# The last 96 MLP features in four column tiles, with a new static plan

## The chip, the cores and the metric

The kernel runs on one core of a Trainium2 chip. Times are microseconds (us) of device time for one launch. The engines are named as in the profile: PE (TensorE) for matrix products and PEld for its weight loads, ACT (ScalarE), DVE (VectorE), POOL (GpSimd) and SP (SyncE), which issues all the DMAs here.

## The reference

With x of 2048 tokens and 512 features, the kernel computes a gated mix of two branches:

```python
x = A_x                                                   # [1, 2048, 512]
g = sigmoid((x * gate_w).sum(-1, keepdims=True))
q, k, v = heads(x @ wqkv)                                 # 32 heads of 16
scores = q @ k.T * 16 ** -0.5                             # only 0 <= i - j < 256 is kept
a = (softmax(scores) @ v) @ wo
h = layernorm(x)                                          # over the features
u = gelu(h.T @ w1 + b1)                                   # [512, 1376], over tokens
y = (u @ w2 + b2).T                                       # [2048, 512]
out = g * a + (1 - g) * y
```

All inputs and outputs are bf16. The MLP mixes tokens: w1 takes the 2048 tokens to F = 1376 hidden features and w2 takes them back. 1376 is 10 times 128 and 96 left over; those 96 are what the change is about.

## The kernel before

**Work and tiles.** Tokens come in NT = 16 tiles of 128. Projections are made per block of 512 tokens and per group of 128 columns (tasks `k`, `q`, `v`). Attention goes by windows of 128 queries, j from -1 to 15; a window has score groups `s` (products of keys and queries, L904 and L924), exponentials `e` on ACT (L949), masks `m` on DVE or POOL (L956 to L988) and outputs `pv` (L1010) that DVE transposes and scales back into the token buffer `xo` (`n1`, `n2`, `nz`, `n3`, `n4`). Score groups of kind C hold two corners of 64 queries and need a mask over the whole tile, which POOL makes in two instructions. Outputs of kind B wait for the C mask too, and for VZ, copies of V that SP's DMAs `vz` put apart; there are three VZ buffers, so a `vz` waits until an earlier window's outputs are done.

The MLP's first half is a loop over NFC = 11 groups of 128 features (L1148): the chain `u{fc}` sums over the 16 token tiles into one bank of PSUM, with a part of w1 as weights and `h` (512 features of x) as the moving operand, and the task `ub{fc}` adds b1 and moves the bank to `ug`. The eleventh, `u10`, has only 96 rows: its 16 products take as long as the others'. One task `gelu` on ACT follows, in four instructions. The second half is a chain `y{t}` per token tile (L1191): 11 products of w2 and `ug` and then 4 of `xo` and `wo`, so that the attention's output projection lands in the same bank. The last tile is made as two halves, y15l and y15r. Task `f{t}` scales the bank by the gate into an output buffer `ot`, and `o{t}` stores it. The ring `ot` has three buffers, so `f` waits for the store three outputs back.

**How a product is issued.** `chain` (L635) cuts its list of products into tasks of two, named after their first index (`u10.4` holds products 4 and 5). A chain task is *flexible*: after a tiled task that is in the set THEN it issues every product as four matmuls of 32 columns, side by side in the array's four column tiles (three for u10's 96 rows); otherwise as one dense matmul:

```python
for c in range(0, rows, 32) if tiled[0] else [0]:
    z_ = c + 32 if tiled[0] else rows
    made.append(nc.tensor.matmul(
        buf(b)[c:z_, c0:c0 + w_], lhsT=lhsT[:, c:z_], rhs=rhs, start=(j == 0), stop=(j == n - 1),
```

Both forms stream the same 512 columns a product; the choice only saves changes of the array's mode. The modes are d (dense), p (128 by 32 tiles, also the outputs pv), s and c (score groups) and h (outputs of corners).

**What sets the order.** Nothing is scheduled at run time. PLAN (L190) lists every task of every engine in its order, written by a planner; `:` gives the buffers or banks that a task takes. `arrange` (L85) replays these lists with the tasks' costs and emits the program in the order of start times. An engine runs its list strictly in order, so a task that waits holds all behind it. That holds for SP's list too: an output store `o8` listed behind `vz12` is issued only when window 10's outputs have given their VZ buffer back.

**Small parts the change touches.** `small_loads` (L252 and on) brings b1, b2 and gate_w into the rows of one tile `biases` by four DMAs (task `bias`), PE transposes it (`biast`), and DVE copies its columns to b1c, b2c and gwc (`biasc`). `junk` is a scratch tile of 128 x 512 that the gate sums `gl` (L803) write and nobody reads.

Of the kernel before, what the change touches and what calls it, by code (L numbers as in the profile page):

```python
# [7 lines left out]
FP32 = mybir.dt.float32  # L8
# [76 lines left out]
def arrange(tasks):  # L85
# [21 lines left out]
    while len(order) < len(tasks):  # L107
# [84 lines left out]
        warm:5 xta0.0.1:6 xta0.0.0:4 warmb xta0.1.0:7 xta0.1.1:5 k1_0.0:0 k1_0.1 k0_0.0:3 k3_0.0:7 q1_0.0:1 k0_0.1  # L192
        q1_0.1 q1_0.2 q3_0.0:6 k1_0.2 k0_0.2 q3_0.1 k3_0.1 q1_0.3 k2_0.0:4 k0_0.3 q1_0.4 q0_0.0:5 q0_0.1 k1_0.3
        q0_0.2 q0_0.3 k0_0.4 q0_0.4 k1_0.4 k3_0.2 k3_0.3 k2_0.1 k2_0.2 k2_0.3 k2_0.4 k3_0.4 q3_0.2 q3_0.3 s1.B0:02
        k3_1.0:4 q2_0.0:5 q3_0.4 k3_1.2 q2_0.1 q0_1.0:7 q0_1.2 q2_0.2 q2_0.3 s0.A0:02 q2_0.4 v1.0:6 q3_1.0:4 v1.2
        q3_1.2 v0.0:7 s0.CNone:20 v0.2 v2.0:6 s-1.CNone:24 v2.2 v14.0:7 v14.2 s2.CNone:02 v12.0:6 biast:4 v12.2
        v13.0:5 v13.2 v3.0:7 s0.A1:02 v3.2 k2_1.0:5 k2_1.2 gate0:4 v5.0:6 v5.2 s1.B1:02 q1_1.0:4 k2_2.0:7 k2_2.2
        pv-1.0:0 v15.0:5 v15.2 q1_1.2 s1.A0:02 k3_2.0:6 k3_2.2 v10.0:7 v10.2 pv0.0:0 pv0.1 pv0.2 s1.A1:24 v8.0:6
        v8.2 v7.0:7 s2.A0:02 v7.2 v4.0:6 k0_2.0:5 v4.2 k0_2.2 k1_1.0:7 s1.CNone:02 k1_1.2 k0_1.0:6 k0_1.2 s2.B0:40
        pv1.0:2 pv1.1 v6.0:7 v6.2 q2_1.0:6 q2_1.2 pv1.2 s2.A1:40 pv1.3 pv1.4 k1_2.0:7 v11.0:6 k1_2.2 v11.2  # L200
        s3.CNone:40 v9.0:7 v9.2 u2.0:6 u2.2 s2.B1:42 u2.4 u3.0:7 u3.2 s3.B0:04 u3.4 u3.6 u3.8 u3.10 pv2.0:2 pv2.1
        s3.A1:04 u3.12 u3.14 u2.6 pv2.2 pv2.3 s3.A0:40 u2.8 u7.0:7 u7.2 s3.B1:24 u7.4 u2.10 u2.12 u7.6 s4.A0:02
        u7.8 u7.10 u7.12 u2.14 u7.14 s4.B0:04 pv3.0:2 q0_2.0:6 q0_2.2 pv3.1 pv3.2 pv3.3 s4.A1:04 q3_2.0:7 u0.0:6
        q3_2.2 s4.B1:20 u0.2 u0.4 u0.6 u0.8 s4.CNone:42 u0.10 u0.12 u10.0:7 s5.A1:40 u0.14 u10.2 u10.4 u10.6
        s5.B0:24 u10.8 u10.10 u10.12 s6.A1:02 u6.0:6 u10.14 pv4.0:4 pv4.1 u6.2 pv4.2 pv4.3 s6.A0:20 u6.4 u6.6 u6.8
        s5.B1:24 q1_2.0:7 q1_2.2 u6.10 u6.12 s5.CNone:20 u6.14 k3_3.0:7 k3_3.2 s5.A0:24 q2_2.0:6 q2_2.2 u5.0:7
        s6.CNone:02 u5.2 u5.4 u5.6 u5.8 s6.B0:40 u1.0:6 pv5.0:2 u1.2 pv5.1 pv5.2 pv5.3 s6.B1:40 u5.10 u1.4 u5.12
        u1.6 s7.A0:42 u5.14 u1.8 pv6.0:0 pv6.1 pv6.2 pv6.3 s7.B0:24 u1.10 u4.0:7 u4.2 s8.A0:02 u4.4 u1.12 u1.14
        u4.6 s7.A1:40 u4.8 k1_3.0:6 k1_3.2 s7.CNone:42 u4.10 u4.12 u4.14 q0_3.0:6 s8.B0:04 q0_3.2 u8.0:7 u8.2
        s8.CNone:20 u8.4 u8.6 u8.8 u9.0:6 s7.B1:24 u8.10 u8.12 u9.2 s8.B1:02 u9.4 u9.6 u9.8 u9.10 u8.14 s8.A1:04  # L210
        pv7.0:2 u9.12 u9.14 pv7.1 pv7.2 pv7.3 s10.A0:60 k2_3.0:4 q2_3.0:5 k2_3.2 q2_3.2 q1_3.0:6 k0_3.0:7 q3_3.0:4
        k0_3.2 q3_3.2 pv8.0:2 pv8.1 pv8.2 pv8.3 q1_3.2 y4.0:5 y0.0:4 y4.2 y0.2 y4.4 y0.4 y0.6 s10.B1:26 y0.8 y0.10
        y0.11 y4.6 y0.13 y4.8 s9.A0:02 y4.10 y4.11 y8.0:4 y8.2 s9.CNone:06 y8.4 y4.13 y8.6 s9.A1:20 y8.8 y8.10
        y8.11 y7.0:5 s9.B1:62 y8.13 y7.2 y7.4 y7.6 s11.B0:60 y7.8 y2.0:4 y7.10 y7.11 s9.B0:62 y7.13 y2.2 y2.4
        s10.A1:60 y9.0:5 y2.6 y2.8 pv9.0:2 pv9.1 pv9.2 pv9.3 s10.B0:60 y2.10 y2.11 y2.13 y9.2 s12.CNone:26 y9.4
# [24 lines left out]
        e10.B0.1 e12.CNone.0:1 e12.CNone.1 e12.A1.0:7 e12.A1.1 e10.CNone.0:6 e10.CNone.1 e11.B1.0:0 e11.B1.1  # L240
        e11.CNone.0:4 e11.CNone.1 e11.A0.0:9 e11.A0.1 e12.B1.0:5 e12.B1.1 e11.A1.0:6 e11.A1.1 e13.A1.0:8 e13.A1.1
# [41 lines left out]
def kernel(  # L283
# [861 lines left out]

    ub = []
    m1 = []
    for fc in range(NFC):  # L1148
        f0 = fc * P
        fsz = min(P, F - f0)  # L1150
        g, w0 = fc // 4, (fc % 4) * P
# [134 lines left out]
```

The softmax here doesn't subtract the row's maximum and nothing guards it: scores larger than these inputs give would overflow.

## Time and profile before

| what | value |
|---|---|
| median of 13 runs | 202.85 us (202.47 to 203.39) |
| the profiled execution: its own time | 202.79 us |
| its span, from the first to the last instruction | 201.0 us |
| granted PE clock, mean | 0.998 |
| instructions | 8987 |
| PE idle by stage: 0 to 10 us | 2.21 us |
| 10 to 140 us | 4.41 us |
| 140 to 160 us | 1.37 us |
| 160 to 190 us | 0.69 us |
| 190 to 201 us | 3.36 us |

The span is shorter than the time by 1.8 us, which lie before the first and after the last instruction. The profile names an instruction by engine and line; since most products come from `chain`, they all have L652, and one tells them apart by what they read: `h,wb` is a `u`, `ug,wb` and `wo,xo` are a `y`, `XT,wqkv` a `k` or `q`, `wqkv,XT` a `v`. Shapes such as `128*32 128x512` are weights (rows by columns) and the moving operand. In the groups, the numbers after the bar are busy time, the mean of one in ns, and the idle time of the engine ahead of them. In the waits, they are the sum, the number of times and the longest. The busy time of PE joins matmuls that overlap.

### The profile page before, as it was taken

The numbers are of one execution on the slowest core, as the hardware profiler recorded it, in microseconds if no ns is written. First come the engines' busy times: TensorE is split into PE (matmuls) and PEld (weight loads), VectorE is DVE, ScalarE is ACT, GpSimd is POOL, SyncE is SP. The second block draws the span as 40 slices with busy tenths as digits, with TensorE's granted clock in tenths as the row PEclk, the third lists the DMA queues.
The fourth block names the chain that finished last, engine by engine and source line by source line (L and its number), as shares of the span: only waits on it lengthen the run. The fifth ranks groups of instructions, "written<-read, shape, count | busy, mean of one in ns | idle before, by whom it ended". The sixth has DMA issues, their size and how long they took to land.

```text
span 201.0 us, 8987 instructions
## 1 busy us (share of the span) xinstructions
PE 188.9 (94%) x4025; PEld 93.7 (47%) x4059; DVE 155.7 (77%) x289; ACT 167.8 (83%) x194; POOL 74.8 (37%) x72
## 2 busy tenths in 40 slices
PE   7899998999999998999999999999998999999993
PEld 3543344343445445446444554334544354544572
DVE  3698959989989982696779688756708986798983
ACT  3278998899899897997899799899796989998651
POOL 6394557724024479226020150202481722007120
PEclk9999999999999999999999999999999999999999
DMA  6999545996023100001199780010030020111101
GB/s 169 274 275 224 134 107 143 362 282 226 3 65 114 33 0 18 18 3 32 37 330 410 262 262 5 0 57 0 31 100 29 29 70 18 54 34 46 43 29 55
DMA packets 23189, 22.02 MB, mean 110 GB/s; under 512 B 7566, under 2 KB 21262, under 8 KB 23150
## 3 DMA queue, kind: packets, MB, share of 16 engines
q1 hardware_dynamic: 23150, 21.44, 36.1%
q8 instruction: 32, 0.52, 1.1%
q14 instruction: 7, 0.06, 0.1%
HBM read 15.61 MB, written 2.10 MB: 88 GB/s over the span
## 4 chain that ended last, share of the span: by engine, by line
PE 82%; DMA 3%; issue 3%; SPq 3%; ACT 3%; POOL 3%; DVE 2%; DVEq 0%
PE pb L652 60%; PE ps L1010 11%; PE ps L924 9%; POOL XT L518 3%; DMA wqkv<-in_A_wqkv_dram 2%; PE ps L904 2%; ACT et L949 1%; DVE ot L423 1%; SPq L711 1%; DMA out_dram<-ot 1%; ACT XT L949 1%; SPq L710 1%; ACT VA L584 1%; SPq L436 0%; DVE XT L1090 0%
## 5 line engine op out<-in xcount | busy, mean ns | idle before, releaser
L949 ACT ACTIVATE et<-ps 128x1024 bf16<-128x1024 f32 (+1 forms) x102 | 95.9, 1001 | 14.2 <-PE ps L924 9.0
L518 POOL TENSOR_SCALAR_AFFINE_SELECT et<-et 128x1024 bf16<-128x1024 bf16 (+2 forms) x34 | 45.1, 1329 | 82.4 <-ACT et L949 49.1
L949 ACT ACTIVATE XT<-ps 128x1024 bf16<-128x1024 f32 (+1 forms) x52 | 49.4, 1011 | 4.0 <-PE ps L924 2.0
L652 PEld LDWEIGHTS <-wb 128*32 128x32 bf16 (+4 forms) x646 | 32.3, 97 | 37.5 <-issue 6.3
L652 PE MATMUL pb<-ug,wb 128*32 128x512 bf16 (+6 forms) x367 | 43.8, 369 | 2.3 <-issue 1.3
L652 PE MATMUL pb<-h,wb 128*32 128x512 bf16 (+2 forms) x260 | 41.3, 380 | 1.6 <-issue 1.6
L652 PE MATMUL pb<-XT,wqkv 128*128 128x512 bf16 (+2 forms) x176 | 30.6, 370 | 2.0 <-issue 1.1
L518 POOL TENSOR_SCALAR_AFFINE_SELECT XT<-XT 128x1024 bf16<-128x1024 bf16 (+2 forms) x11 | 16.6, 1510 | 29.5 <-ACT XT L949 25.0
L924 PE MATMUL ps<-QZ,KT 32*128 32x256 bf16 (+1 forms) x528 | 23.9, 262 | 0.1
L1010 PEld LDWEIGHTS <-VA 128*32 128x32 bf16 (+1 forms) x1056 | 20.4, 97 | 6.9 <-issue 3.2
L736 DVE TENSOR_TENSOR QZ<-pb,par 128x1024 bf16<-128x1024 f32 x16 | 19.4, 1214 | 5.2 <-PE pb L652 5.1
L423 DVE TENSOR_SCALAR ot<-pb,c,c 128x512 bf16<-128x512 f32 (+1 forms) x15 | 11.8, 785 | 11.8 <-PE pb L652 11.6
L1010 PE MATMUL ps<-et,VA 128*32 128x128 bf16 (+2 forms) x736 | 19.2, 217 | 0.2 <-ACT et L949 0.2
L652 PEld LDWEIGHTS <-wqkv 128*128 128x128 bf16 (+1 forms) x184 | 12.3, 97 | 14.4 <-issue 1.1
L1090 DVE STREAM_TRANSPOSE et<-ps 128x1024 f32<-128x1024 f32 (+1 forms) x12 | 14.4, 1203 | 5.8 <-PE ps L1010 5.2
L924 PEld LDWEIGHTS <-KT 32*128 32x128 bf16 x528 | 7.8, 92 | 20.8 <-ACT et L949 7.8
L652 PE MATMUL pb<-wo,xo 128*32 128x512 bf16 (+2 forms) x161 | 17.1, 375 | 0.2
L652 PE MATMUL pb<-wqkv,XT 128*128 128x512 bf16 x60 | 15.9, 380 | 0.6 <-issue 0.5
L985 DVE TENSOR_TENSOR et<-et,mask 128x1024 bf16<-128x1024 bf16 x17 | 13.2, 783 | 1.5 <-ACT et L949 1.5
L1010 PEld LDWEIGHTS <-VZ 128*32 128x32 bf16 x832 | 13.3, 98 | 0.9 <-issue 0.5
L752 DVE BATCH_NORM_STATS2 stats<-xo 128x6 f32<-128x512 bf16 x16 | 10.5, 677 | 2.5 <-DMA xo<-in_A_x_dram 2.5
L1125 DVE STREAM_TRANSPOSE xo<-zt 128x512 bf16<-128x512 bf16 (+1 forms) x17 | 11.4, 673 | 0.3
(76 smaller groups left out, 186.8 us busy)
## 6 DMA issues: line engine op xcount, KB each, us to landing
wb<-in_B_w_dram SPq DMA_DIRECT2D x8, 512.0 KB, 9.3
wb<-in_B_w_dram SPq DMA_DIRECT2D x2, 2048.0 KB, 8.0
out_dram<-ot SPq DMA_DIRECT2D x15, 128.0 KB, 2.4
VZ<-VA SPq DMA_DIRECT2D x26, 70.0 KB, 2.7
xo<-in_A_x_dram SPq DMA_DIRECT2D x3, 512.0 KB, 5.6
wb<-in_B_w_dram SPq DMA_DIRECT2D x4, 352.0 KB, 6.0
wqkv<-in_A_wqkv_dram SPq DMA_DIRECT2D x4, 256.0 KB, 5.3
wb<-in_B_w_dram SPq DMA_DIRECT2D x1, 1024.0 KB, 5.1
```

Of the source, the lines that this page charges most:

```text
L423: return nc.vector.tensor_scalar(out=out_, in0=in_, scalar1=scale, scalar2=bias, op0=ALU.mult, op1=ALU.add)
L518: return nc.gpsimd.affine_select(out=out_, in_=in_, pattern=[[0, n] for n in pattern] + [[step, HB]], compare_op=op, fill=0.0, base=base_, ...
L652: made.append(nc.tensor.matmul(buf(b)[c:z_, c0:c0 + w_], lhsT=lhsT[:, c:z_], rhs=rhs, start=(j == 0), stop=(j == n - 1), skip_group_check= ...
L736: lambda k=k, b=b: nc.vector.tensor_tensor(out=QZ[:, k, :, (i % NQ) * SB:(i % NQ + 1) * SB], in0=buf(b)[:, None, :].to_broadcast([P, 2, SB ...
L752: f"bs{t_}", {"DVE": 0.67}, lambda b=b, t_=t_: nc.vector.bn_stats(buf(b)[:], xo[:, t_, :]),
L904: made.append(nc.tensor.matmul(buf(b2[r // 2])[m_:m_ + HB, at:at + P], lhsT=keys(t_, k)[rows, a:a + HB], rhs=q[rows], start=True, stop=Tru ...
L924: made.append(nc.tensor.matmul(to[:, :, done:done + m], lhsT=keys(t_, k)[rows], rhs=q[rows], start=True, stop=True, tile_position=(32 * r, 0),
L949: lambda n_=n_: nc.scalar.activation(out=shape(buf(e)[:, n_ * 1024:(n_ + 1) * 1024]), in_=shape(buf(b2[n_])), func=ACT.Exp, scale=SCALE),
L985: return nc.vector.tensor_tensor(out=view, in0=view, in1=mask[:, "AB".index(x), None, :].to_broadcast([P, n_, HB]), op=ALU.mult)
L1010: return lambda: nc.tensor.matmul(to(), lhsT=v() if callable(v) else v, rhs=buf(e)[rows, col:col + n], start=first, stop=last, tile_positi ...
L1090: lambda: nc.vector.transpose(out=view(buf(tr).bitcast(FP32)), in_=view(buf(o))), [last], takes=[tr], uses=[o],
L1125: return nc.vector.transpose(out=to, in_=src)
```

## The change

The eleventh group leaves the loop and is made by hand. Its 96 features are three groups of 32. Column tiles 0, 32 and 64 of the array each take one group and stream only the first 384 of the 512 columns; the fourth tile, at 96, which had nothing to do before, makes the last 128 columns of all three groups, one after another, into different columns of the same bank. So a step has six matmuls. Eight tasks of two steps stay in "p" mode always. The bank then has the last quarters in partitions 96 to 127, so DVE moves it out in four instructions, and the 96 biases are needed once more, in rows of 32 that lie at columns 96 to 127 of `biases`: one more small DMA, and b1c has 14 columns.

The ring `ot` gets `junk` as a fourth buffer, which comes free when the last `gl` has run. And all five lists and THEN are written anew: nearly every task has a new place or bank, and some have a new engine.

The core of the diff (of the lists, only stretches that the prediction speaks of):

```diff
 PLAN = dict(
     PE="""
...
-        q3_2.2 s4.B1:20 u0.2 u0.4 u0.6 u0.8 s4.CNone:42 u0.10 u0.12 u10.0:7 s5.A1:40 u0.14 u10.2 u10.4 u10.6
-        s5.B0:24 u10.8 u10.10 u10.12 s6.A1:02 u6.0:6 u10.14 pv4.0:4 pv4.1 u6.2 pv4.2 pv4.3 s6.A0:20 u6.4 u6.6 u6.8
...
-        y0.11 y4.6 y0.13 y4.8 s9.A0:02 y4.10 y4.11 y8.0:4 y8.2 s9.CNone:06 y8.4 y4.13 y8.6 s9.A1:20 y8.8 y8.10
-        y8.11 y7.0:5 s9.B1:62 y8.13 y7.2 y7.4 y7.6 s11.B0:60 y7.8 y2.0:4 y7.10 y7.11 s9.B0:62 y7.13 y2.2 y2.4
-        s10.A1:60 y9.0:5 y2.6 y2.8 pv9.0:2 pv9.1 pv9.2 pv9.3 s10.B0:60 y2.10 y2.11 y2.13 y9.2 s12.CNone:26 y9.4
...
+        u0.2 q3_2.0:6 q3_2.2 s4.B0:42 u0.4 u0.6 u0.8 u0.10 s4.CNone:04 u10.0:6 u0.12 u0.14 u10.2 s6.A0:20 u10.4
+        u10.6 u10.8 u10.10 s5.B1:42 u6.0:7 u6.2 u10.12 u6.4 s6.B0:40 u10.14 u6.6 pv4.0:2 pv4.1 pv4.2 pv4.3 s5.A0:04
...
+        y0.13 y4.6 y4.8 s9.A0:04 y8.0:7 y8.2 y4.10 y4.11 s9.B0:02 y4.13 y8.4 y8.6 s10.CNone:40 y7.0:6 y8.8 y8.10
+        y7.2 s9.CNone:42 y8.11 y8.13 y7.4 y7.6 s9.B1:40 y7.8 y2.0:7 y2.2 s11.CNone:24 y7.10 y7.11 y7.13 y2.4
+        s10.B0:02 y2.6 y2.8 pv9.0:4 pv9.1 pv9.2 y2.10 pv9.3 s10.A1:20 y9.0:6 y2.11 y2.13 s10.B1:42 y9.2 y9.4 y9.6
...
     POOL="""
...
-        m8.B1 m9.A0 m11.B0 m10.A1 m10.B1 m12.C m11.C m13.A1 m12.A0 m14.C m15.ANone
...
+        m8.A0 m8.B1 m9.C m10.A1 m11.C m10.B0 m10.B1 m11.B1 m11.A1 m12.B0 m12.A0 m12.A1 m13.C m15.ANone
...
     SP="""
...
-        x0.0 x0.2 wqk0 wqk1 wqk2 wqk3 x1.4 xt1 wv x2.8 bias xt3 x3.12 vs0 w1_20 xt2 vs2 vz2:0 vs1 gw w1_10 w1_21
...
-        w2_2 wo vz9:0 o4 o0 o2 vz11:0 vz12:2 vs13 o8 o7 o1 o5 o10 vz13:0 o3 o11 vz14:1 o6 o12 o9 o13 o14 o15l o15r
...
+        x0.0 x0.2 wqk0 wqk1 wqk2 wqk3 x1.4 xt1 wv bias xt3 w1_02 x2.8 vs0 x3.12 xt2 w1_03 w1_12 vs1 w1_13 w1_00
...
+        w2_2 vz13:2 o0 o4 vz9:1 vz10:0 o8 o7 o2 o9 o1 vz11:1 vz12:0 o5 vs13 o10 vz14:1 o3 o11 o12 o6 o13 o14 o15l
...
     mask = sb.tile([P, 7, HB], BF16, name="mask")
     par = sb.tile([P, 2], FP32, name="par")
     gwc = sb.tile([P, 4], BF16, name="gwc")
-    NB = NFC + NT + 4
+
+    N1 = NFC + 3
+    NB = N1 + NT + 4
     biases = sb.tile([NB, P], BF16, name="biases")
     gwr = sb.tile([P, D], BF16, name="gwr")
     junk = sb.tile([P, D], BF16, name="junk")
-    b1c = sb.tile([P, NFC], FP32, name="b1c")
+    b1c = sb.tile([P, N1], FP32, name="b1c")
     b2c = sb.tile([P, NT], FP32, name="b2c")
     mv = sb.tile([P, NT, 2], FP32, name="mv")
     rstd = sb.tile([P, NT], FP32, name="rstd")
...
     ztr = ring("zt", 2, [P, D], BF16)
     rdr = ring("rd", 2, [P, 32], FP32)
     otr = ring("ot", 3, [P, D], BF16)
+
+    otr.tiles.append(junk)
+    otr.avail.append(None)
+    jb = Buf(otr)
+    jb.index = 3
     vzr = Ring("vz", [VZ[:, i] for i in range(NVZ)])
 
     def buf(b):
...
             nc.sync.dma_start(
                 biases[NFC - 1:NFC, 0:F - (NFC - 1) * P], B_b1[(NFC - 1) * P:F].rearrange("(o p) -> o p", o=1)
             ),
-            nc.sync.dma_start(biases[NFC:NB - 4, :], B_b2[:].rearrange("(t p) -> t p", p=P)),
+            nc.sync.dma_start(
+                biases[NFC:N1, P - 32:P], B_b1[(NFC - 1) * P:F].rearrange("(g p) -> g p", p=32)
+            ),
+            nc.sync.dma_start(biases[N1:NB - 4, :], B_b2[:].rearrange("(t p) -> t p", p=P)),
             nc.sync.dma_start(biases[NB - 4:NB, :], gate_w.rearrange("(t p) -> t p", p=P)),
         ]
 
...
         keep(mask[HB:P, 6, :], mask[HB:P, 6, :], [], "F")
 
     k2 = add("masks", {"POOL": 4.2}, masks)
-    dbias = add("bias", {"SP": 1.5}, small_loads, [k0], lat=2.5)
+    dbias = add("bias", {"SP": 1.8}, small_loads, [k0], lat=2.5)
     bb = bank("xt")
     bt = add(
         "biast", {"PE": 0.12},
...
     )
 
     def bias_columns():
-        nc.vector.tensor_copy(out=b1c[:], in_=buf(bb).bitcast(BF16)[:, 0:NFC])
-        nc.vector.tensor_copy(out=b2c[:], in_=buf(bb).bitcast(BF16)[:, NFC:NB - 4])
+        nc.vector.tensor_copy(out=b1c[:], in_=buf(bb).bitcast(BF16)[:, 0:N1])
+        nc.vector.tensor_copy(out=b2c[:], in_=buf(bb).bitcast(BF16)[:, N1:NB - 4])
         return nc.vector.tensor_copy(out=gwc[:], in_=buf(bb).bitcast(BF16)[:, NB - 4:NB])
 
     k3 = add("biasc", {"DVE": 0.5}, bias_columns, [bt], uses=[bb])
...
                         out=junk[:], in0=xo[:, t_, :], scalar=1.0, in1=gwr[:], op0=ALU.mult, op1=ALU.mult,
                         accum_out=ez[:, t_:t_ + 1],
                     ),
-                    [dx[t_], dgw], two=True,
+                    [dx[t_], dgw], uses=[jb], two=True,
                 ))
             lready += gt
             gm = add(
...
 
     ub = []
     m1 = []
-    for fc in range(NFC):
+    for fc in range(NFC - 1):
         f0 = fc * P
-        fsz = min(P, F - f0)
+        fsz = P
         g, w0 = fc // 4, (fc % 4) * P
         mms = [(w1[g][:, t_, w0:w0 + fsz], h[:, t_, :], fsz) for t_ in range(NT)]
         b, t = chain(f"u{fc}", mms, dw1[g] + hready, "u")
...
             lambda b=b, fsz=fsz, fc=fc: affine(ug[:fsz, fc, :], buf(b)[:fsz, :], None, b1c[:fsz, fc:fc + 1]),
             [t, k3], uses=[b],
         ))
+
+
+
+    bl = bank("u")
+    W3 = 3 * D // 4
+    gl, wl = (NFC - 1) // 4, ((NFC - 1) % 4) * P
+
+    def emit_last(t_):
+        return [
+            nc.tensor.matmul(
+                buf(bl)[to:to + 32, c0:c0 + w], lhsT=w1[gl][:, t_, wl + 32 * n:wl + 32 * n + 32], rhs=h[:, t_, a:a + w],
+                start=(t_ == 0 and n == first), stop=(t_ == NT - 1), tile_position=(0, to), skip_group_check=True,
+            )
+            for n, to, c0, a, w, first in
+            [(n, 32 * n, 0, 0, W3, n) for n in range(3)] + [(n, 96, n * P, W3, P, 0) for n in range(3)]
+        ]
+
+    last = None
+    for t_ in range(0, NT, 2):
+        last = add(
+            f"u{NFC - 1}.{t_}", {"PE": 0.33}, lambda t_=t_: emit_last(t_) + emit_last(t_ + 1),
+            dw1[gl] + hready if last is None else [last], takes=[bl] if last is None else [],
+            uses=[] if last is None else [bl], mode="p", ins=24,
+        )
+    m1.append(last)
+
+    def move_last():
+        made = []
+        for to, n, c0, a, w in [(0, 96, 0, 0, W3)] + [(32 * n, 32, n * P, W3, P) for n in range(3)]:
+            at, col = (0, NFC - 1) if n == 96 else (96, NFC + to // 32)
+            made.append(nc.vector.tensor_scalar(
+                out=ug[to:to + n, NFC - 1, a:a + w], in0=buf(bl)[at:at + n, c0:c0 + w],
+                scalar1=b1c[at:at + n, col:col + 1], scalar2=None, op0=ALU.add,
+            ))
+        return made
+
+    ub.append(add(f"ub{NFC - 1}", {"DVE": 1.35}, move_last, [last, k3], uses=[bl]))
 
     cuts = [(0, 3), (3, 7), (7, NFC - 1)]
 
```

## The prediction

> **What bounds the kernel now.** I read the busy shares first, then the chain that ended last by engine, then who TensorE (PE) waited for.
>
> ```profile
> PE 188.9 (94%) x4025; PEld 93.7 (47%) x4059; DVE 155.7 (77%) x289; ACT 167.8 (83%) x194; POOL 74.8 (37%) x72
> ```
> ```profile
> PE 82%; DMA 3%; issue 3%; SPq 3%; ACT 3%; POOL 3%; DVE 2%; DVEq 0%
> ```
> ```profile
> PE pb L652 <- issue: 4.4, 28, 0.2
> PE pb L652 <- DVE ot L423: 0.9, 1, 0.9
> PE ps L1010 <- POOL XT L518: 0.4, 1, 0.4
> ```
>
> PE is busy for 188.9 of 201.0 us and is 82% of the chain, so array time saved anywhere after the first loads comes off the end, unless another engine is late next. Only two waits in the middle exceed 0.3 us. The 4.4 us of "issue" are 28 pieces of 0.16 us: such a stretch lacks exactly one matmul (5 records in 1.24 us after the gap, 6 in 1.40 us without one), so I take them as missing records, not time to win.
>
> Next, the chain in order of time, which gives prices.
>
> ```profile
> 71.63 2.61 POOL XT L518
> 74.30 2.46 POOL XT L518
> 76.80 0.58 PE ps L1010 x44
> ...
> 80.71 1.84 PE pb L652 x32
> ...
> 82.94 1.41 PE pb L652 x24
> ...
> 162.43 1.36 PE ps L1010 x128
> ```
>
> A dense product over 128 rows in "p" mode is four matmuls side by side, so x32 is 8 steps and x24 is 6. The two differ by 0.43 us over 2 steps: **0.215 us a step of 512 columns**, and 1.84 - 8 x 0.215 = **0.12 us to enter a mode**. Dense stretches give the same (1.83 us for 8, 1.40 us for 6; 0.11 us entry). The last line is one block's outputs: 128 matmuls, 3072 columns on each of the four column tiles, 3072 / 512 x 0.215 = 1.29 us, so almost all of it is streaming. The first lines show pv4.1 held by the two halves of a POOL mask.
>
> The groups with shapes kept apart give the object of the change and a row like its new one:
>
> ```profile
> L652 PE MATMUL pb<-h,wb 128*96 128x512 bf16 x14 | 3.5, 382 | 0.0
> L1010 PE MATMUL ps<-et,VZ 128*32 128x64 bf16 x384 | 6.9, 193 | 0.0
> ```
>
> The timeline shows the other wait:
>
> ```profile
> 149.18 6.24 SPq L1216 DMA_DIRECT2D out_dram<-ot  x3
> ...
> 151.20 0.81 DVE L423 TENSOR_SCALAR ot<-pb,c,c 128x512 bf16<-128x512 f32 x1 [5.14 <-PE pb L652]
> ...
> 152.07 0.60 PE L652 MATMUL pb<-ug,wb 128*128 128x512 bf16 x2 [0.94 <-DVE ot L423]
> ```
>
> The 151.20 line is f9, although y9 had been finished since about 149.6. It needs output buffer 2, whose store o8 was queued on SP behind vz11, vz12 and vs13 and went at 149.18 (f8 was done at 144.08); stores land after 2.4 us. PE then waits for f9's bank with y5.
>
> **What the Trainium skill says.**
> - "TensorEngine Tiling (Array Packing)", Key Properties: tiles work independently, and a change of tiling mode drains the array. The trace agrees: 0.11 to 0.12 us an entry.
> - The same page, Restrictions: column tiling excludes Fast Weight Load. So would three short matmuls in a row on one tile show their weight loads? In the blocks' outputs each tile takes new weights every 64 columns, 27 ns, and still streams at 1.29 of 1.36 us: loads of 32 columns are hidden there.
> - "TensorE: Matmul & The Clock Gate", Step-by-step: weight loads are pulled ahead of running matmuls when they go to the background buffer, matmuls stay in order. PEld's 97 ns loads beside uninterrupted PE agree.
> - "SBUF — State Buffer", SBUF: two separate sides: VectorE and GpSimd take a shared port pair as an exclusive lock. The mask pair took 5.12 us at 71.63, beside VectorE work, and 4.29 us at 146.18, where VectorE was nearly idle; that fits.
>
> **The change, part by part.**
>
> *Array time of u10.* Before: 16 steps of 512 columns (14 dense, 2 in three column tiles), 16 x 0.215 = 3.45 us. After: each step has 384 columns on tiles 0 to 2 and three times 128 on tile 96, so 384 columns on every tile: 384 / 512 x 0.215 = 0.162 us, 2.59 us in all. Gain **0.86 us**. Lower bound of the cost is 2.59. Upper: each of the three loads on tile 96 shows its 97 ns, 3 x (54 + 97) = 0.45 us a step, 7.25 us. I take the low end because of the 27 ns above.
>
> *Mode entries.* u10 must now run in "p". I counted runs of equal mode in the two PE lists: 171 become 173 (d 58 to 56, p 32 to 36). 4 x 0.12 - 2 x 0.11: **+0.25 us**.
>
> *Instructions.* u10 has 96 pairs of load and matmul instead of 20, and 81 other steps are tiled instead of 74: about 240 more instructions on 8084. The output blocks issue 256 in 1.36 us without a wait in the trace, against u10's 192 in 2.6 us. I take 0; the bounds are 0 and 0.3 us.
>
> *Moving u10 out.* One ACT instruction (0.69 us) becomes four on DVE: from the ot rows, 0.81 us for 512 columns and 0.54 for 256, I estimate 0.67 + 3 x 0.35 = 1.7 us. DVE is 77% busy, and gelu is far behind u10, with five more u groups between: 0 on the path. Without that cover, 1 us. Other copies change sides (ACT gives ten and takes seven; DVE gives three masks net to POOL): a few us on engines with slack, 0.
>
> *Bias.* The fifth small DMA is one more issue of about 0.3 us on SP, ahead of xt3, x2.8, vs0, x3.12 and xt2. But bias now goes before x2.8 (0.5 us) and so xt3 leaves no later than before, at about 12.7 us. xt2, after vs0 as before, leaves at about 21.3 us; its first user v10 comes at about 28.3 us by adding up the list, against a landing of 26.4 (traffic ended 5.1 us after issue before) to 29.4 (8.1, the longest transpose). I take 0, bounds 0 and 1.1. The wider b1c copy is 3 columns: nothing.
>
> *Fourth output buffer.* junk is free once the gl sums are done, long before the first output. f5, f7, f12 and f15l use it, and on SP o8, o7, o2, o9 and o1 now stand ahead of vz11, vz12 and vs13. The store that held f9 goes before those waits: **-0.94 us**. Bounds: -0.94 and 0, if PE merely waits elsewhere. Behind vz12, which waits for pv10, there is now o5, whose buffer is next needed by f12: covered by over 10 us.
>
> *The moved POOL mask.* m4.C stays; between s4.C and pv4.1 there are now 12 steps of u0 and u6 (2.59 us), u10 (2.59), three score groups (0.99), pv4.0 (0.22) and six entries (0.7), 7.1 us, against 24 steps (5.17), the same groups and pv4.0 and four entries (0.46), 6.8 us, before. **-0.25** of the 0.41, bounds -0.41 and 0. But m9.C moves from DVE (about 1.3 us) to POOL (4.3 to 5.1). From the end of s9.C to pv9.1 the new list has 25 steps (5.38), s9.B1, s11.C and s10.B0 with their entries (1.04), pv9.0 (0.22) and four other entries (0.45): 7.1 us. The mask needs 0.13 + 1.94 (two exponentials) + 0.06 + 4.3 to 5.1 = 6.4 to 7.25 us. I take **+0.2 us**, with ACT prompt; bounds 0 and 2.1, if ACT lags a pair.
>
> *All the rest planned anew.* Streaming (608 products, 60 + 17 score groups, 16.8 us of outputs) comes to about 166.6 us by these prices, 171 entries to 20; PE's 190.9 us from 6.80 to 197.7 leave some 4 us of waits, of which 1.35 are the two named. A new order keeps the same total work but breaks the pairs of wait and cover that the old one had. I put **+0.9 us** for new small waits, an estimate: three quarters of the 1.19 us of waits that I take out. Bounds 0 and 3. The start (first wqkv piece at 6.80) and the tail after pv15 (15 half-width products and y14's last four, 2.5 us, cover the DVE's 2.3 us from pv15 to y15's last inputs) are alike.
>
> *Sum.* 202.79 - 0.86 + 0.25 - 0.94 - 0.25 + 0.20 + 0.9 = **202.1 us**, against the profiled execution's own 202.79 (span 201.0 and 1.8 around it); the median of the runs, 202.85, is 0.06 from it. The runs spread over 0.9 us, so a change under about 0.2% (0.4 us) can't be told from none.
>
> **The rivals.**
> - *The new order has few waits of its own:* only the terms with a place count, 202.1 - 0.9 = **201.2**. For it: the longest PE wait goes. Against it: ACT is 19.15 of 20 us busy from 120 to 140 us; little slack for a list that reshuffles everything. 10%.
> - *A wash:* new waits of 1.7 us, not 0.9, eat all, **202.9**. For it: some 2.6 us of small waits exist even in the present order. 22%.
> - *Slower: m9.C on POOL decides.* Right after gelu (4.7 us and two table loads of 1.28 on ACT) the exponentials e9.A0, e9.B0, e10.C, e9.C come at a rate of one pair (1.94 us) per some 2 us of PE work. If ACT is one pair behind at s9.C, the mask ends 1.94 us later and pv9.1 waits 2.1 us instead of 0.2: 202.1 + 1.9 = **204.0**. It makes the kernel slower by over 0.4 us from a lag of about 1.2 us. For it: ACT nearly full in that stage. Against it: before, ACT waited for PE (0.43 us) at 127.46, so it had caught up. 25%.
> - *The fourth tile serves no purpose:* tile 96's loads show (7.25 us instead of 2.59), **206.8**. Against it: the 27 ns rows. 3%.
>
> **How the numbers follow.** Likeliest at 202.1 (between 201.4 and 202.4): 40%. Faster by over 0.2%: 40 + 10 = 50%; within: 22%; slower: 25 + 3 = 28%. The range runs from 200.9 (the first rival, less the 0.3 us by which entries and pv9 may cost less) to 204.2 (the third, plus the rest of pv4's wait), leaving out the last and the tails, under 2 in 10. Faster holds the most, but not by much; the likeliest case's own range is 201.4 to 202.4.
>
> **What would show it.** In the changed profile, u10's chain pieces: 12 matmuls per two steps in 0.33 us right, 0.9 us if loads show. PE's list of waits should have no DVE ot entry near 150 us; a POOL mask entry at L1010 near pv9, over 1 us, is the third rival. If PE is busy for about 0.6 us less yet the span isn't shorter, the new order's waits have it, and the idle time per stage tells where. I am wrong if the sum of PE's idle time in the middle grows by more than 1.5 us.

## The result, and the profile after

The median of 11 runs is **205.37 us** (204.75 to 207.06) against 202.94 us for 48 runs of the kernel before on the same chip: a ratio of **1.013, interval 1.0113 to 1.0147**. The kernel became slower by about 2.6 us; I had forecast 202.1 us, faster, with a range to 204.2. Executions that were disturbed (a lower clock, or a time well above the fastest of the same kernel) are left out of the ratios but not of the medians; in e1 below they are three of six, and its trace is of one of them. The profiled execution took 205.06 us (span 203.3), 2.27 us more than before's 202.79.

The page after, busy shares and the chain by engine:

```profile
PE 190.5 (94%) x4150; PEld 95.1 (47%) x4180; DVE 158.3 (78%) x292; ACT 166.7 (82%) x191; POOL 79.7 (39%) x75
...
PE 71%; DVE 15%; DMA 6%; issue 3%; POOL 2%; ACT 1%; SPq 0%; POOLq 0%
```

PE held 82% of the chain before and DVE 2%. Now DVE holds 15% and DMA 6%: some 30 us of the chain ran through VectorE and 12 us through transfers. The busy shares hardly show it (DVE 77 to 78%). PE's waits after the start:

```profile
PE pb L662 <- issue: 3.8, 24, 0.2
PE ps L934 <- ACT et L959: 1.6, 3, 0.6
...
PE ps L1020 <- DMA VZ<-VA: 0.8, 1, 0.8
PE pb L662 <- DVE QZ L746: 0.5, 1, 0.5
PE ps L934 <- DVE ug L429: 0.3, 1, 0.3
...
PE pb L662 <- DVE ug L429: 0.2, 1, 0.2
```

Both waits that I had taken out are gone from this list: no `ot` and no POOL entry. New are the score groups (L934) that wait for ACT, one transfer of VZ, and DVE entries.

u10 itself is as forecast. The groups of after, with shapes apart:

```profile
L1179 PE MATMUL pb<-h,wb 128*32 128x128 bf16 x48 | 3.5, 220 | 0.0
L1179 PE MATMUL pb<-h,wb 128*32 128x384 bf16 x48 | 3.5, 328 | 0.0
```

The timeline of PE in after:

```profile
71.04 1.52 PE L1179 MATMUL pb<-h,wb 128*32 128x384 bf16 x48
72.50 0.40 PE L934 MATMUL ps<-QZ,KT 32*128 32x256 bf16 x8
```

Forty-eight matmuls are eight steps, and the next group starts 1.46 us after the first of them. Less one mode entry of 0.12 that is 1.34 us, so 0.16 to 0.17 us a step, without loads that show.

**Where the time came from.** For both kernels I summed the work ahead of every score group with the prediction's prices and compared it with the times at which the groups started. What the clock says beyond the work is called lost. The entries are estimates: the prices are rounded, so a change in the last column may be off by 0.2 to 0.3 us.

| stretch (us in after) | lost before | lost after | change |
|---|---|---|---|
| ahead of the first score group | 6.81 | 6.55 | -0.26 |
| to s4.C (68.7) | 1.02 | 0.50 | -0.52 |
| s4.C to s5.A1 (85.8); in before, s4.C to s6.A0 (78.6) | 0.88 | 2.90 | **+2.02** |
| from there to s10.A0 (117.0) | 0.29 | 1.79 | **+1.50** |
| s10.A0 to s15.B (192.5) | 1.65 | 1.39 | -0.26 |
| after s15.B | | | +0.37 |
| work (prices) | | | -0.60 |

The sum is +2.25 of the 2.27 us. The work, by the same prices, fell as forecast (-0.61). Two stretches make the kernel slower. The busy column is no help: PE's busy time *rose* by 1.6 us with less work. I put this down to the ends of matmuls, which the profile models, so that part of a wait counts as busy. Its idle time from 10 to 190 us grew by only 1.15 us (6.48 to 7.63).

**First stretch, 72 to 86 us.** The timeline of after, first DVE's part:

```profile
72.12 1.92 DVE L1117 TENSOR_TENSOR zt<-et,rd 128x512 bf16<-128x512 f32 x1
73.97 0.70 DVE L1135 STREAM_TRANSPOSE xo<-zt 128x512 bf16<-128x512 bf16 x1
74.70 1.86 DVE L1117 TENSOR_TENSOR zt<-et,rd 128x512 bf16<-128x512 f32 x1
76.60 0.71 DVE L1135 STREAM_TRANSPOSE xo<-zt 128x512 bf16<-128x512 bf16 x1
77.23 1.69 DVE L1200 TENSOR_SCALAR ug<-pb,b1c 96x384 bf16<-96x384 f32 x4
```

POOL's part, the two halves of m4.C:

```profile
71.39 4.64 POOL L528 TENSOR_SCALAR_AFFINE_SELECT XT<-XT 64x2048 bf16<-64x2048 bf16 x2 [0.29 <-ACT XT L959]
```

ACT's part, the exponentials e5.B1 and e6.B0:

```profile
74.14 1.94 ACT L959 ACTIVATE et<-ps 128x1024 bf16<-128x1024 f32 x2 [1.04 <-DVE zt L1117]
76.66 1.94 ACT L959 ACTIVATE et<-ps 128x1024 bf16<-128x1024 f32 x2 [0.58 <-DVE zt L1117]
```

And PE's, the score groups s6.B0, s5.A0 and s5.B0:

```profile
75.22 0.40 PE L934 MATMUL ps<-QZ,KT 32*128 32x256 bf16 x8 [0.58 <-ACT et L959]
...
78.65 0.40 PE L934 MATMUL ps<-QZ,KT 32*128 32x256 bf16 x8 [0.38 <-ACT et L959]
...
81.09 0.40 PE L934 MATMUL ps<-QZ,KT 32*128 32x256 bf16 x8 [0.63 <-ACT et L959]
```

Read it from below. PE's score groups s6.B0, s5.A0 and s5.B0 wait for exponentials. The exponentials e5.B1 (74.14) and e6.B0 (76.66) wait for DVE's `zt` products: these are n31 and n33, which read the et buffers 3 and 0 that e5.B1 and e6.B0 are to fill. In the kernel before, the same operation took 0.69 us twice (69.51 and 71.56, in the fence below); here it takes 1.92 and 1.86 us, 2.4 us more in all. POOL's mask m4.C has two halves, 71.39 to 73.51 and 73.57 to 76.03; n31 ends 0.54 us after the first and n33 0.53 us after the second. Behind them on DVE come ub10, u10's four moves (77.23), and the next products. The kernel before, DVE:

```profile
69.51 0.69 DVE L1107 TENSOR_TENSOR zt<-et,rd 128x512 bf16<-128x512 f32 x1
...
71.56 0.69 DVE L1107 TENSOR_TENSOR zt<-et,rd 128x512 bf16<-128x512 f32 x1
...
73.57 1.20 DVE L1107 TENSOR_TENSOR zt<-et,rd 128x512 bf16<-128x512 f32 x1
78.85 1.25 DVE L1090 STREAM_TRANSPOSE XT<-ps 128x1024 f32<-128x1024 f32 x1 [4.08 <-PE ps L1010]
```

Before, one product met the mask (1.20) and DVE then stood idle for 4.08 us. The windows from 70 to 85 us (length; DVE's busy time and instructions; clock, DMA share, GB/s), in the kernel before:

```profile
70.00:85.00 15.00, 9.09 (x20) 1.00 0.05 12
```

and in the kernel after:

```profile
70.00:85.00 15.00, 14.66 (x28) 1.00 0.02 4
```

So DVE has next to no idle time left here, and 2.4 of its 14.66 us are the two products' lengthening.

**Second stretch, 112 to 117 us.** The chain of after:

```profile
104.13 0.37 SPq L1231
...
104.55 10.25 DMA VZ<-VA
...
114.85 0.74 PE ps L1020 x44
```

SP's queue in the timeline of after:

```profile
98.90 5.61 SPq L1231 DMA_DIRECT2D wb<-in_B_w_dram  x2
104.55 0.52 SPq L720 DMA_DIRECT2D VZ<-VA  x1
```

vz7, two copies of 70 KB, was issued behind two w2 loads of 2 MB each and landed 10.25 us later; pv7 waited for it, and a late ub8 then held s10.A0. Before, vz7 went ahead of the w2 loads: its first copy left at 91.28 us and landed at 93.83. SP's queue in the kernel before:

```profile
91.28 0.46 SPq L710 DMA_DIRECT2D VZ<-VA  x1
...
99.59 12.62 SPq L1184 DMA_DIRECT2D wb<-in_B_w_dram  x3
```

### The profile page after: what moved, and what is told of

Same layout as the page of the kernel before. It is cut to its first block, busy times and chain, and to the rows that moved or that the text cites. A ratio compares the mean times of both kernels' runs of the same rounds, so it can differ in the third digit from the quotient of the medians.

```text
span 203.3 us, 9231 instructions
## 1 busy us (share of the span) xinstructions
PE 190.5 (94%) x4150; PEld 95.1 (47%) x4180; DVE 158.3 (78%) x292; ACT 166.7 (82%) x191; POOL 79.7 (39%) x75
## 4 chain that ended last, share of the span: by engine, by line
PE 71%; DVE 15%; DMA 6%; issue 3%; POOL 2%; ACT 1%; SPq 0%; POOLq 0%
PE pb L662 52%; PE ps L1020 9%; PE ps L934 7%; DMA VZ<-VA 5%; DVE zt L1117 3%; DVE junk L814 2%; POOL et L528 2%; PE ps L914 2%; DVE QZ L746 2%; DVE xo L1135 1%; DMA xo<-in_A_x_dram 1%; DVE ug L429 1%; DVE et L1100 1%; DVE rd L1108 1%; DVE ug L1200 1%
## 5 line engine op out<-in xcount | busy, mean ns | idle before, releaser
L528 POOL TENSOR_SCALAR_AFFINE_SELECT et<-et 128x1024 bf16<-128x1024 bf16 (+3 forms) x34 | 45.8, 1358 | 89.9 <-ACT et L959 51.2
L959 ACT ACTIVATE XT<-ps 128x1024 bf16<-128x1024 f32 x50 | 48.3, 1024 | 4.7 <-PE ps L934 3.6
L662 PEld LDWEIGHTS <-wb 128*32 128x32 bf16 (+2 forms) x713 | 30.7, 96 | 34.5 <-issue 7.5
L662 PE MATMUL pb<-ug,wb 128*32 128x512 bf16 (+4 forms) x404 | 44.8, 370 | 0.8 <-issue 0.6
L662 PE MATMUL pb<-h,wb 128*32 128x512 bf16 (+1 forms) x295 | 38.4, 380 | 1.4 <-issue 1.4
L528 POOL TENSOR_SCALAR_AFFINE_SELECT XT<-XT 128x1024 bf16<-128x1024 bf16 (+1 forms) x14 | 20.8, 1488 | 21.4 <-DVE et L1104 6.3
L1100 DVE STREAM_TRANSPOSE et<-ps 128x1024 f32<-128x1024 f32 (+1 forms) x15 | 17.7, 1178 | 12.4 <-PE ps L1020 9.3
L934 PE MATMUL ps<-QZ,KT 32*128 32x256 bf16 (+1 forms) x528 | 24.0, 262 | 1.9 <-ACT et L959 1.6
L934 PEld LDWEIGHTS <-KT 32*128 32x128 bf16 x528 | 8.0, 92 | 22.2 <-ACT et L959 13.0
L430 DVE TENSOR_SCALAR ot<-pb,c,c 128x512 bf16<-128x512 f32 (+1 forms) x12 | 9.3, 779 | 9.5 <-PE pb L662 9.5
L662 PE MATMUL pb<-wqkv,XT 128*128 128x512 bf16 (+1 forms) x66 | 15.8, 380 | 0.6 <-issue 0.6
L1117 DVE TENSOR_TENSOR zt<-et,rd 128x512 bf16<-128x512 f32 (+1 forms) x15 | 14.4, 959 | 0.3
```

The lines of the kernel that those rows point to most:

```text
L430: return nc.vector.tensor_scalar(out=out_, in0=in_, scalar1=scale, scalar2=bias, op0=ALU.mult, op1=ALU.add)
L528: return nc.gpsimd.affine_select(out=out_, in_=in_, pattern=[[0, n] for n in pattern] + [[step, HB]], compare_op=op, fill=0.0, base=base_, ...
L662: made.append(nc.tensor.matmul(buf(b)[c:z_, c0:c0 + w_], lhsT=lhsT[:, c:z_], rhs=rhs, start=(j == 0), stop=(j == n - 1), skip_group_check= ...
L934: made.append(nc.tensor.matmul(to[:, :, done:done + m], lhsT=keys(t_, k)[rows], rhs=q[rows], start=True, stop=True, tile_position=(32 * r, 0),
L959: lambda n_=n_: nc.scalar.activation(out=shape(buf(e)[:, n_ * 1024:(n_ + 1) * 1024]), in_=shape(buf(b2[n_])), func=ACT.Exp, scale=SCALE),
L1100: lambda: nc.vector.transpose(out=view(buf(tr).bitcast(FP32)), in_=view(buf(o))), [last], takes=[tr], uses=[o],
```

## Experiments

**Theory.** The two stretches are the loss: vz7 queued behind w2, and DVE late between 72 and 86 us because products on DVE that read two SBUF tiles wait for POOL's mask and hold et buffers. **Rivals:** u10's new form costs time in itself (its 152 more instructions, its moves on DVE); or DVE simply has too much work there, mask or not. A side question is whether the fourth output buffer was worth its 0.94 us. All ratios are to the kernel before, run on the same chip beside them.

### vz7 ahead of w2

```diff
-... w2_0 w2_1 vz7:2 vz8:1 w2_2 ...
+... vz7:2 vz8:1 w2_0 w2_1 w2_2 ...
```

> The changed kernel with vz7 and vz8 issued ahead of w2_0 and w2_1 on SP. Theory C (pv7.1's wait is the 70 KB of vz7 standing behind 4 MB of w2 in the DMA queues, 10.2 us from issue to landing): vz7 lands before 103 us, PE's 0.81 us wait goes, 204.5 us, 0.8 to 1.1 under the changed kernel's 205.4; some 0.4 us stay, for s10.A0 needs u8's bank cleared. Rival D (pv7 waits for something else that ends at the same time, a mask or an exponential): no change, 205.4.

Measured: 203.27 us, ratio **1.0062 (1.004 to 1.0084)** against after's 1.013: 1.4 us less, where 0.8 to 1.1 had been expected. The wait for VZ is gone from PE's list, and the loss ahead of s10.A0 fell from 1.54 to 0.40 us. What stays there is the wait for ub8. This part of the theory is shown.

### The mask m4.C and the DVE products: five runs

m4.C from POOL to DVE, behind n33:

> The changed kernel with the mask m4.C (4.6 us in two POOL instructions) made on DVE behind n33 (1.2 us). Theory E (between 72 and 86 us PE waits for ACT, ACT for buffers that DVE gives back late, and DVE is late because POOL's mask holds the shared port while n31, n33 and nz4 want it, 1.92, 1.86 and 0.98 us instead of 0.69, 0.69 and 0.2): n31 and n33 take 0.7 us, 1.5 to 2.2 us of the 2.8 us of waits go, 203.2 to 203.9. Rival F (DVE simply has too much to do there, ub10 among it): 1.2 us more for DVE, 205.4 to 206.5.

Measured: 204.3 us, 1.0116 (1.0083 to 1.0149), which can't be told from after's 1.013. The timeline of this kernel has n31 and n33:

```profile
72.85 0.67 DVE L1117 TENSOR_TENSOR zt<-et,rd 128x512 bf16<-128x512 f32 x1
...
74.18 0.69 DVE L1117 TENSOR_TENSOR zt<-et,rd 128x512 bf16<-128x512 f32 x1
```

So it is the mask on POOL that lengthens the two products, as the theory has it. The first loss fell from 0.65 to 0.27 us, but new waits for DVE (0.6 at the gate sums) took its place. What the lengthening costs stays open here, since the mask now adds 1.2 us to DVE.

So I made the mask short instead, on top of vz7 early:

```diff
-return [keep(view[HB * i:HB * i + HB], view[HB * i:HB * i + HB], [32], "DF"[i]) for i in range(2)]
+w = 1 if j == 4 else 32
+return [keep(view[HB * i:HB * i + HB, 0:w], view[HB * i:HB * i + HB, 0:w], [w], "DF"[i]) for i in range(2)]
```

> The kernel after with vz7 and vz8 ahead of the w2 loads (as e2), and the POOL mask m4.C cut to the first of its 32 column groups, so that 31/32 of that one mask is left out and POOL is done with it in under 0.5 us instead of 4.64. Theory L (the lock of the shared port): n31 and n33 take 0.7 us each instead of 1.92 and 1.86, DVE is 2.4 us earlier, the losses between 72 and 86 us fall from 2.83 to under 1 us: 201.0 to 201.8 us. Rival (the amount of DVE work, not the lock): n31 and n33 stay long or the PE losses stay above 2 us: 202.7 to 203.3 us.

Measured: 201.70 us, **0.9972 (0.9952 to 0.9993)**: 1.8 us less than with vz7 early alone, faster than before. The timeline of this kernel, DVE:

```profile
72.52 1.26 DVE L1117 TENSOR_TENSOR zt<-et,rd 128x512 bf16<-128x512 f32 x1
73.71 0.70 DVE L1135 STREAM_TRANSPOSE xo<-zt 128x512 bf16<-128x512 bf16 x1
74.44 0.69 DVE L1117 TENSOR_TENSOR zt<-et,rd 128x512 bf16<-128x512 f32 x1
```

n33 is back at 0.69 us; n31, at 1.26, met the next mask (72.10 to 73.25). No score group waits for ACT any more, and from s4.C to s5.B0 0.47 us are lost instead of 2.17. So with this mask left out the stretch costs almost nothing, with the same work on DVE: a full DVE alone doesn't make the loss.

Then three attempts to have it with the mask whole. f3 moves n31 ahead of the mask:

```diff
-n32:1 ez1 nz1:0 nz3:1 ub0 n31:0 n42 n33:1
+n32:1 nz1:0 n31:0 ez1 nz3:1 ub0 n42 n33:1
```

> The kernel after with vz7 and vz8 ahead of the w2 loads (as e2, 203.3 us) and, on DVE, n31 moved ahead of ez1, so that it runs before the POOL mask m4.C starts and gives et buffer 3 back at about 71.0 instead of 74.05 us; n33 follows ub0 and n42. Theory L (n31 and n33 slowed by the mask hold the et buffers of e5.B1 and e6.B0, and PE's score groups wait for that): the losses of 0.65, 0.71, 0.70 and 0.77 us between 72 and 86 us shrink to less than 1.2 us together: 201.0 to 202.0 us. Rival (DVE has simply too much to do there, 15.8 us of work in 15 us, and what is moved back is waited for in its turn): 202.7 to 203.5 us.

Measured: 203.50 us, 1.0034 (1.0008 to 1.006). That is in the rival's range, and its interval overlaps that of vz7 early alone. n31 took 0.69 us and e5.B1 started at 72.7, but ub0 had slipped, and PE's timeline shows the wait that took the place:

```profile
74.32 1.05 PE L661 MATMUL pb<-h,wb 128*32 128x512 bf16 x16 [1.68 <-DVE ug L428]
```

So ub0 went ahead of ez1 as well:

> The kernel after with vz7 and vz8 early and n31 ahead (as f3), but ub0 directly behind n31 and ahead of ez1. In f3 PE waited 1.68 us for ub0, which had been moved behind ez1 and nz3. Theory L (that wait took the place of the 2.8 us): u6 no longer waits, s6.B0 neither, and what stays is e6.B0, held by n33 until the mask ends at about 76 us: losses between 72 and 86 us of 1.0 to 1.7 us against 2.83 in e2 and about 2.2 in f3; 201.7 to 202.6 us. Rival (DVE's amount of work decides): losses of 2.2 us or more, 202.8 us or above.

Measured: 204.46 us, 1.0073 (1.0048 to 1.0099), no better than vz7 alone; the theory's number missed, and the rival's came true. n31 ended at 71.5 and e5.B1 was on time, but n33 still met the mask (74.20 to 76.22, 2.02 us), e6.B0 started at 76.31 as ever, and from s4.C to s5.A1 2.92 us were lost, as in e2 (2.90). The end of n33, not of n31, sets this stretch: 7.9 us after s4.C in e2 and in g2, 6.0 us in f4.

And m4.C on DVE besides:

> The kernel of g2 with the mask m4.C besides taken from POOL and put on DVE behind n33. No POOL mask then holds the shared port while n31 and n33 run, and n31, n33 and m4.C (1.25 us) are all done by about 76 us. Theory L: losses between 72 and 86 us under 1.3 us, 201.4 to 202.3 us. Rival (DVE's amount of work decides, now 1.25 us more): losses above 2.2 us, 202.8 us or above.

Measured: 204.56 us, 1.0089 (1.0059 to 1.0119); the theory missed and the rival's number came true again. The timeline of this kernel, POOL's masks, then n31 and n33:

```profile
67.19 4.88 POOL L527 TENSOR_SCALAR_AFFINE_SELECT et<-et 128x1024 bf16<-128x1024 bf16 x4 [3.52 <-ACT et L958]
```
```profile
71.04 1.57 DVE L1116 TENSOR_TENSOR zt<-et,rd 128x512 bf16<-128x512 f32 x1
...
75.26 0.69 DVE L1116 TENSOR_TENSOR zt<-et,rd 128x512 bf16<-128x512 f32 x1
```

n31 did meet a POOL mask, against the expectation: without m4.C POOL goes straight on to m4.B1, which ends at 72.07, and n31 ends at 72.61. n33 now took 0.69 us, but it ended at 75.95, only half a microsecond earlier counted from s4.C (7.4), and m4.C pushed ub10 and what follows back by 1.2 us: 3.42 us lost.

What follows from the five: leaving the mask out gains 1.8 us (f4), and n31 and n33 are long only where they meet a mask on POOL. Both sides of the argument are needed, since DVE is full in this stretch: whatever lengthens its products is waited for, and none of the four runs with the whole mask gained clearly. That the 1.8 us run through these products, and not through the mask's own end, is argued: f4 also ends the mask earlier, but in e2, which still has it, PE's list shows no wait for POOL. An order that keeps n33 clear of the mask wasn't found.

### The store o8 earlier, in the kernel before

```diff
-o4 o0 o2 vz11:0 vz12:2 vs13 o8 o7
+o4 o0 o2 o8 vz11:0 vz12:2 vs13 o7
```

> The kernel before with the store o8 one place before vz11 in SP's list, nothing else. Theory G (f9, and PE with y5, waited for o8, which stood behind vz11, vz12 and vs13): f9 starts at about 149.9 us instead of 151.2, PE's 0.94 us wait goes, 202.0 us. Rival H (PE meets the next wait at once): 202.7 to 202.9.

Measured: 201.23 us, **0.9954 (0.9933 to 0.9976)**, 0.93 us less than before: the price that I gave the fourth buffer holds, and the old kernel could have had it by moving one name.

### u10 alone, and the blocks of PE's instructions

The kernel before with only the new u10: the loop's last group by hand, the fifth bias DMA, ub10 on DVE behind n31; all lists else unchanged.

> The kernel before with u10 in four column tiles and nothing else: the old lists, the old three output buffers, the fifth bias DMA, and ub10 moved from ACT to DVE behind n31. Theory A (the new lists lose the time, u10 itself gains): 16 steps of 0.162 us instead of 0.215, 0.86 us less, two more entries into tiled mode at 0.12 us, so 202.3 us, 0.6 us under the kernel before. Rival B (u10's form or its four moves on DVE cost more than they gain): 203 us or above.

Measured: 1.0331 (1.0298 to 1.0364), some 6.7 us slower. Both expectations missed by far. PE stood still in the middle of output blocks while waiting for nothing that the profile shows. The page of the kernel before lists the queue that brings instructions (packets, MB, share):

```profile
q8 instruction: 32, 0.52, 1.1%
```

That is 32 packets of 16 KB; PE left 8117 records before, 31.7 times 256. The Trainium skill, "Runtime: NRT & Kernel Launch", Instruction fetch mechanics, says that instructions come in 16 KiB blocks of 256 and that crossing into a new block is mostly hidden. The runs below do not bear out the second of these. u10's 152 additional instructions shift all block ends behind it into other work, and theory F is that this makes the 6.7 us. Two runs test it. f2 leaves u10 as it was and puts 76 pairs of small dummies ahead of it, the same 152 instructions; f1 adds 52 pairs to e1, so that the shift is 256 and all stands in its block as before. The dummies write one column of u10's bank, which u10 then overwrites; the cut shows those of f1.

```diff
+nc.tensor.matmul(
+    buf(b)[32 * (i % 4):32 * (i % 4) + 32, 0:1], lhsT=w1[gl][:, 0, wl:wl + 32], rhs=h[:, 0, 0:1],
+    start=True, stop=True, tile_position=(0, 32 * (i % 4)), skip_group_check=True,
+)
```

> The kernel before, u10 unchanged, with 76 pairs of weight load and one-column matmul ahead of u10's first step: the same 152 instructions more as e1, but neither u10's new form nor its moves on DVE. Theory F (block boundaries of the instruction stream): PE stops without a wait at the same places as in e1, 208 to 211 us. Rival (u10's form or its moves): only the pads are paid, 152 at 1.36 us per 256 (0.8 us) to 1.5 us: 203.0 to 203.7 us.

> This is the run of the kernel before with u10 alone in column tiles (e1), plus 52 pairs of weight load and one-column matmul ahead of u10's first step. PE's list of instructions is then longer than before's by 152 + 104 = 256, so that all after u10 stands at the same place within its block of 256 instructions as in the kernel before. Theory F (e1's 8 us are waits at block boundaries of PE's instruction stream): the gaps without a wait go, DVE catches up, and the time is that of before, less 0.6 us for u10, plus the pads, 104 instructions at 1.36 us per 256 (0.55 us) or somewhat more: 202.1 to 203.2 us. Rival (u10's form, its moves on DVE or the longer list as such cost the 8 us): 210 to 211.5 us.

Measured: f2 210.91 us, **1.0427 (1.0383 to 1.0471)**; f1 202.81 us, **1.0018 (0.9998 to 1.0039)**. Adding 104 instructions to e1 made it 6.3 us faster, so neither u10's form nor its moves cost the time. PE's waits in f2:

```profile
PE pb L658 <- issue: 4.6, 29, 0.2
PE ps L1016 <- issue: 4.0, 5, 1.0
PE pb L658 <- DVE ot L423: 3.1, 1, 3.1
```

The place of one of the five in PE's timeline of f2:

```profile
167.86 0.23 PE L1016 MATMUL ps<-et,VZ 128*32 128x64 bf16 x8
169.06 0.24 PE L1016 MATMUL ps<-et,VA 128*32 128x128 bf16 x4 [0.97 <-issue]
```

PE's waits in f1:

```profile
PE pb L655 <- issue: 4.6, 29, 0.2
...
PE pb L655 <- DVE ot L423: 0.6, 1, 0.6
PE ps L1013 <- POOL XT L521: 0.5, 1, 0.5
```

The L655 and L658 "issue" rows are the missing records of before. The L1016 row is the stall: five pieces of up to 1 us inside runs of outputs, which f1 hasn't. Numbered in order, PE's records in f2 (loads, matmuls and a few others) stop at 3503, 5288, 6308, 7328 and 7839: the distances are 7, 4, 4 and 2 times 255 (one record over). A block is 256 instructions, of which one seems to leave no record: over the first three distances, 15 blocks, there are 16 matmuls fewer than loads. The stalls are 1.0, 0.6, 1.2, 1.1 and 1.1 us from start to start, 5.0 in all (the L1016 row counts 4.0 of them, from the modelled ends). Some 2.2 us more come from f9's wait, 3.1 us instead of 0.9, I take it because SP's stores stand behind copies that wait for the late outputs. Together that is most of the 7.7 us by which the span grew. A stall came where 256 instructions had passed in 2.5 to 4.2 us, the stall counted in; other short passages (2.07 us at 114.7, 1.69 at 179.1, 3.15 at 91.5) went without one, so how far ahead blocks are fetched stays open.

So what extra instructions cost depends on where they move the block ends: 152 of them cost some 8.6 us in f2, and 256 next to nothing in f1, where every end lies as the old order has it. The planner of this kernel counts the blocks (`arrange` has BLOCK = 256). The kernel after, planned with them, has just three such gaps, at block ends: from start to start 0.46 us at 159.40, 0.28 at 168.32 and 0.34 at 194.70, where 0.2 us is the usual distance of two steps, so some 0.4 us in all. The one at 194.70 is 0.14 of the 0.37 us lost after s15.B; the rest of these is not explained.

Last, what u10 is worth with the blocks kept, without the pads' own time, and with o8 early:

```diff
+    s4.B1 s4.CNone s5.A1 pv5.0
     pv0.0 pv0.2 s2.B0 pv1.0 pv1.2 ...
```

> The kernel before with u10 alone in column tiles (as e1), with o8 one place ahead of vz11 on SP, and with PE's list 256 instructions longer than before's as in f1, but almost without pads: eight pairs of steps that stand beside u10 or pv5.0 in dense mode are tiled (12 instructions more for each, the same streaming), and four pairs of pads make up the rest. Four mode entries go with it (0.4 us). Theory F with u10 worth 0.6 us: before with o8 early stood at a ratio of 0.9954, and from it come 0.6 us for u10 and up to 0.4 us for the entries, less up to 0.3 us for waits on the POOL mask at pv4: 200.2 to 201.2 us where before is at 202.3. Rival (u10's gain is lost again in waits of ACT and DVE): 201.3 to 202 us. Rival (any other place of the blocks stalls): above 203 us.

Measured: 201.52 us where before is at 202.82, **0.9937 (0.9915 to 0.996)**, inside theory F's range. That is the lowest ratio of all, but only 0.35 us ahead of o8 early alone, and the intervals overlap. The prices give 1.04 us less work than before (u10, and two mode entries fewer); PE's wait for POOL's mask at pv4.1 grew from 0.4 to 0.9 us and took half of that, probably since u10 stands right ahead of pv4, so that what it saves is waited for there.

## Why the prediction was wrong, point by point

- **u10's array time, -0.86:** right, 0.16 to 0.17 us a step. **Entries, +0.25:** the work as a whole fell by 0.60 where the two terms say 0.61.
- **Instructions, 0 (0 to 0.3):** too low. About 0.4 us in the kernel after, and 6.7 us for e1. My argument, that blocks of outputs issue 256 in 1.36 us without a wait, was true only where no block end falls at a bad place, which is what the old order had seen to. The kernel says so itself: `arrange` counts PE's instructions in blocks of 256.
- **Moving u10 out, 1.7 us on DVE and 0 on the path:** the size was right (1.64), the place not: the chain of after runs through ub10 at 77.31 to 78.92. I took DVE's 77% over the whole span as slack; in these 15 us it became 14.66 of 15.
- **Bias, 0:** the start lost 0.26 us less than before; not followed up.
- **Fourth buffer, -0.94:** right; the wait is gone, and o8 early shows 0.93 us in the kernel before.
- **pv4's mask, -0.25:** the wait is gone altogether, but partly because PE comes later.
- **pv9's mask on POOL, +0.20:** 0.36 us lost there; m9.C took 4.64 us. The chain of after has it:

```profile
137.86 2.12 POOL et L528
...
140.04 2.46 POOL et L528
...
142.54 0.81 PE ps L1020 x60
```

- **"All the rest planned anew", +0.9 (0 to 3): this step failed.** I sized new waits from the waits that I took out and didn't look for them in the new lists. They came to 1.5 us at vz7 and 2.9 us between 72 and 86 us, where 0.9 lay before. Both could be read. The diff shows vz7 behind w2_0 and w2_1, 4 MB, where it had stood ahead of them, and before's trace had the duration of such loads (three issues in 12.62 us from 99.59). And I cited the Trainium skill's "SBUF — State Buffer", SBUF: two separate sides, for what the lock does to POOL's masks, but not for what the same section says of a DVE operation with two SBUF inputs, that it is blocked while POOL has the port. Before's own n31 took 1.20 us beside m4.C against 0.69 for its like, and the new DVE list puts n31 and n33 both there, with an et buffer behind each. `arrange` has this wait too (`port`). The copies that change sides, "a few us on engines with slack, 0", are the same error.

With both causes away (f4) the kernel stands at 0.9972 of before, 202.3 us for 202.85, against the forecast 202.1. That is near the forecast by luck in part: 202.1 holds the +0.9 for new waits, and the terms with a place alone give 201.2. So some 1.1 us of other losses remain in f4, among them 0.4 us at ub8 and 0.36 at pv9 (where I had +0.20). f4 leaves out most of one mask, so it gives a bound on what that cause costs and is not a version of the kernel. Of the rivals the third had the right sign, with too small a size (204.0) and the wrong place: gelu and m9.C weren't it. My own criterion, idle time of PE up by more than 1.5 us, reads 1.15 by busy time and 2.74 by starts; the starts are the ones to use.

Open: why some short passages through a block don't stall, whether an order exists that keeps n33 clear of m4.C at no cost, and where the rest of the 0.37 us after s15.B goes.

## What to carry to other kernels

When a change brings a new order, read the new lists for each buffer that one engine frees and another waits for, in the stage in question, and for each small transfer that now stands behind a large one; a lump sum for "new small waits" is no estimate. Engine shares belong to a stage, not to the span. A list of instructions tuned around its 256-instruction blocks isn't free to grow: a change that adds instructions ahead of tiled work can cost many times what it saves (here 6.7 us for 0.86), and padding to a whole block shows in one run whether that is the reason.

## What the runs showed of the hardware that I had not expected

- In f2, PE stopped for 0.6 to 1.2 us at five ends of 256-instruction blocks in runs of tiled outputs, where a block had passed in 2.5 to 4.2 us, though not at every such place; 152 dummy instructions cost 4.3% (f2), 256 more than before cost 0.2% along with u10's gain (f1).
- A DVE product of two SBUF inputs that starts beside a POOL mask ends half a microsecond after the mask's instruction: 1.9 us instead of 0.69, twice in a row, once for each half of the mask; the same 0.53 to 0.54 us show in before, f3, f4, g2 and g3.
- A copy of 70 KB behind 4 MB in the same queue landed after 10.25 us; ahead of them, one took 2.55 us.
